# Batch 1 of a Fourier-mixing and ELU kernel in the quarter form, with another order of the first 17 steps

## The chip, the cores and the metric

The kernel runs on one core of one Trainium2 chip. The metric is the device time of one execution in microseconds. A profile of one execution on the chip, with a trace of every instruction, goes with it. In the text PE is TensorE (matmuls), DVE is VectorE, ACT is ScalarE, POOL is GpSimd, and SP is the engine that issues most transfers.

## The reference

```python
batch, seq, dim = (8, 3008, 256)
X = np.fft.fft(x, axis=1)
X = np.fft.fft(X, axis=2)
y = X.real.astype(np.float32).reshape(8 * 3008, 256)
h = y @ w_in                              # 256 x 2048
g = np.where(h > 0.0, h, np.exp(np.minimum(h, 0.0)) - 1.0)
out = (g @ w_out).astype(np.float32)      # 2048 x 256
```

The real part of a two-dimensional Fourier transform of every batch, and then a two-layer network with ELU between its layers. All of it is float32.

## The kernel before

**What is computed, and in what pieces.** The transform is symmetric, so only half of its rows (1504 in a batch) are made, as a real part (`Rr`, with one channel kept apart in `Rb`) and an imaginary part (`Ir`); each of them gives two tokens, h+ and h−. The channel part of the transform is folded into the first weight matrix: `fold_chunk` multiplies w_in by cosines and sines, chunk by chunk (eight chunks, 256 of the 2048 hidden columns each), into `Wc` and `Ws`. `Rr`, `Ir` and `Rb` are rings of columns in SBUF which the transform fills and the main loop reads. The middle channel's weights, one row of `Ws`, are needed as columns, `wex`: `spread_last_row` takes them there by two SP transfers through DRAM, `turn_last_row` and `put_last_row` by two one-column matmuls against the tile `pick` and an ACT copy.

**The main loop.** A tile is 256 ring columns, and has eight steps, one for each chunk. Step i is: P (`mm_P`, two matmul instructions of Wc by Rr into a PSUM bank of the tag H), E on DVE (`even_part`, L1352, `Rb * wex + H` into SBUF, in two halves), Q (`mm_Q`, Ws by Ir onto the same bank, so that H becomes h+), h− on DVE (L1366, `2E − H`), the ELU of both (b+ and b− and x+ and x− on ACT; g+ and g− on DVE, L1382), four sums on GpSimd (L603, G<-G), and the matmuls of the second layer into pA to pD. From the third tile on these are a Winograd form of seven products (X1, X2, X3); in the first 16 steps they are plain (Xa, Xb). Three banks have the tag H, and transforms and folds use them too.

**The transform of a batch.** It has four parts (real and imaginary, even and odd k), each in an even and an odd half. Batches 0 and 1 use the class `Dft`: rows of x in four tiles `xl0` to `xl3` (128 x 1536, `load_x`), folded on GpSimd by `mirror_folds` (30 operations for batch 1), then a matmul half of three instructions with 128 rows (`dft_mms`), of 189 columns for an even half and 377 for an odd one. Batches 2 to 7 use the class `Quarter`: the rows come in two sets, near and far, 96 and 94 rows of four (`load_quarter` with indirect transfers, `load_odd`), go through `mirror_sum`, `half_sum` (on DVE), `channel_fold`, `channel_edge`, and then `quarter_pairs`, `shift_pairs` and `turn_pairs` (on DVE, with the table `twist_tab`), and each half is four instructions with 94 or 95 rows and columns. `at_quarter` places a transform of that form: two halves, then the step at which its far part is finished and the step at which its even and odd half are joined.

**The extra channel.** One channel of all eight batches is transformed by itself: `load_ext` and `get_ext` bring it, `fold_ext` folds it, `dft_ext` (24 matmul records) transforms it, four ACT copies `ext_side` take it from PSUM, `ext_unfold`, `ext_rows`, `ext_up` and `ext_down` unfold it, and `spread_ext` puts it into the rings by SP transfers through DRAM.

**What sets the order.** `at(t, fn)` files an operation under a time t; all are sorted by t and issued in that order. A step is T = `PERIOD` = 4.8 long in these times. Operations on the compute engines are pinned to the order of the program; transfers on SP that are not pinned may be moved by the scheduler. The order until about step 7 is a list written out, `FRONT`, with short names: P4 is P of step 4, f3 the fold of chunk 3, Wc3 and Ws3 ACT's copies of that fold out of PSUM, J a part of batch 0's last transform, w3… and u3… the conversions of weight chunks. The words of a line are filed 0.001 apart.

Of the kernel before, what the change touches and what calls it, by code (L numbers as in the profile page):

```python
# [9 lines left out]
FP = mybir.dt.float32  # L10
# [167 lines left out]
def kernel(  # L178
# [381 lines left out]
    def load_quarter_mats(ri, kodd):  # L560
        t = cpool.tile([128, BW], FP, tag=f"MC{ri}{kodd}", name=f"QM{ri}{kodd}")
        QM[ri, kodd] = t
        n = sum(QW[i % 2] for i in range(2 * ri + kodd))
        nc.sync.dma_start(
            out=t[0:96, 0 : QW[kodd]], in_=QM_dr.ap()[:, n : n + QW[kodd]]
        )
# [166 lines left out]
    def mirror_folds(L):  # L733

        ops = []
        rows = [t.rearrange("p (m d) -> p m d", d=ND) for t in L]
        for j, k in ((3, 2), (0, 1)):
            own, other = rows[j], rows[k][:, ::-1]
            for m in range(6):
                ops.append(  # L740
                    lambda own=own, other=other, m=m: gtt(
                        own[:, m, 1:], own[:, m, 1:], other[:, m, :0:-1], ALU.add
                    )
                )
            ops.append(
                lambda own=own, other=other: gtt(
                    own[:, :, 0:1], own[:, :, 0:1], other[:, :, 0:1], ALU.add
                )
            )
        EO = [None] * 4  # L750
        for kodd in range(2):
            z = L[1 + kodd]
            for n in range(4):
                c = slice(384 * n, 384 * n + 384)
                ops.append(
                    lambda z=z, c=c, kodd=kodd: gtt(
                        z[:, c], L[0][:, c], L[3][:, c],
                        ALU.subtract if kodd else ALU.add,
                    )
                )  # L760
            for ri in range(2):
                t = EO[2 * ri + kodd] = spool.tile(
                    [128, 768], FP, tag=f"{'eo'[ri]}{1 + 2 * kodd}", bufs=1, name="eo"
                )
                for h in range(2):

                    def fold(z=rows[1 + kodd], t=t, ri=ri, h=h):
                        src = z[:, 3 * h : 3 * h + 3]
                        lo, hi = (
                            v.rearrange("p m (d o) -> p m o d", o=2)  # L770
                            for v in (src[:, :, 1:129], src[:, :, 255:127:-1])
                        )
                        o = t[:, 384 * h : 384 * h + 384]
                        o = o.rearrange("p (m o d) -> p m o d", o=2, d=64)
                        if ri:
                            gtt(o, lo, hi, ALU.subtract)
                        else:
                            gtt(o, lo[:, :, ::-1], hi[:, :, ::-1], ALU.add)

                    ops.append(fold)  # L780
                if not ri:
                    o = t.rearrange("p (m o d) -> p m o d", o=2, d=64)
                    state["edge", kodd] = lambda o=o, z=rows[1 + kodd]: act(
                        o[:, :, 0, 63:64], z[:, :, 0:1]
                    )
        return EO, ops

# [12 lines left out]
    def half_sum(kodd, far, h):  # L800

        n = 94 if far else 96
        a, b, o = (lines(j, far)[0:n] for j in (0, 3, 1 + kodd))
        for m in (2 * h, 2 * h + 1):
            vtt(o[:, 3 - m], a[:, m], b[:, m], ALU.subtract if kodd else ALU.add)
# [440 lines left out]
    def ext_side(g, rows=NB):  # L1246
        kodd, par = EXT[g]
        n = NO if kodd else NE if par else 2 * NH
        t = spool.tile([128, 384], FP, tag="side", bufs=2, name="side")
        act(t[0:rows, 0:n], state["ext"][32 * g : 32 * g + rows, 0:n])  # L1250
        state["side", par] = t

    def ext_unfold(kodd, tt, rows=NB):
        n = NO if kodd else NE
        h = (n + 1) // 2
        even = state["side", 0]
        a = spool.tile([128, NE], FP, tag="bs", bufs=BS, name="bs")
        unfold(a, even, even[:, h : 2 * h], rows, n, tt)
        state["es"] = a[0:rows]

    def ext_rows(kodd, tt, rows=NB):
        n = NO if kodd else NE
        if not kodd or rows < NB:
            rx = spool.tile([128, HALF + 1], FP, tag="rx", bufs=1, name="rx")
            state["rx"] = rx[0:rows]
        rx, a, b = state["rx"], state["es"], state["side", 1][0:rows]
        o, base = 1 - kodd, kodd * RUN
        m = n - 2 * o
        tt(rx[:, base : base + n], a[:, 0:n], b[:, 0:n], ALU.add)
        top = base + RUN - 1  # L1270
        tt(rx[:, top : top - m : -1], a[:, o : o + m], b[:, o : o + m], ALU.subtract)
        if not kodd:
            tt(rx[:, HALF:], a[:, 0:1], b[:, 0:1], ALU.subtract)
            nc.sync.dma_start(
                out=r4_dr.rearrange("o b -> b o"), in_=rx[:, HALF : HALF + 1]
            )
        nc.sync.dma_start(
            out=r128_dr[0:rows, base : base + RUN], in_=rx[:, base : base + RUN]
        )

    def ext_up():
        rx = state["rx"] = spool.tile(
            [128, HALF + 1], FP, tag="rx", bufs=1, name="rx"
        )[0:NB]
        a, b = state["es"], state["side", 1][0:NB]
        vtt(rx[:, 0:NE], a, b[:, 0:NE], ALU.add)
        vtt(rx[:, HALF:], a[:, 0:1], b[:, 0:1], ALU.subtract)

    def ext_down():
        rx, a, b = state["rx"], state["es"], state["side", 1][0:NB]  # L1290
        vtt(
            rx[:, RUN - 1 : RUN - 1 - (NE - 2) : -1],
            a[:, 1 : NE - 1], b[:, 1 : NE - 1], ALU.subtract,
        )
        nc.sync.dma_start(
            out=r4_dr.rearrange("o b -> b o"), in_=rx[:, HALF : HALF + 1]
        )
        nc.sync.dma_start(out=r128_dr[0:NB, 0:RUN], in_=rx[:, 0:RUN])
# [398 lines left out]
    def open_x(b):  # L1697
        state["L"], state["loads"] = load_x(b)

# [47 lines left out]
    names["L"] = lambda: [open_x(1)] + [state["loads"][n]() for n in (4, 5)]  # L1747
    for n in range(4):
        names[f"L{n}"] = lambda n=n: state["loads"][n]()
    for slot in range(8):  # L1750
# [10 lines left out]
        (-20.84, "e3 o3"),  # L1761
        (-19.11, "w0a w0b w0p w0R c3"),
        (-17.62, "w0s w0M"),
        (-16.21, "e0a e2b o2"),
        (-14.32, "e2a o0 c2"),
        (-12.89, "E2 f0 O2"),
        (-11.63, "xl1 xs e1 x-even"),
        (-9.8, "e0b c1 o1 c0 x-odd x-copy Wc0"),
        (-8.58, "E0 Ws0 EO0"),
        (-7.29, "wm0 wex0 O0 R-odd"),  # L1770
        (-5.76, "w1b EO2"),
        (-4.55, "w2b R-even u0b w2d u0a EO1 w1d"),
        (-3.25, "I-odd R-copy w1l w1a x-sum u0l"),
        (-1.92, "w1R R-sum w1p I-even x-down R-up"),
        (-0.64, "Irc2 w1s u0p P0 x-up I-copy w1M"),
        (0.82, "R-down O-even Irc I-sum u1l V0"),
        (2.21, "w1P w2l P1 I-up u0d"),
        (3.48, "I-down Q0 u0R R4 V1"),
        (4.76, "f1 h0 b+0 O-copy u0s Q1"),
        (5.99, "x+0 w2a b-0 u0M O-odd"),  # L1780
        (7.24, "Wc1 g+0 x-0 O-sum Ws1"),
        (8.46, "w2R w2p h1 wm1 g-0 b+1 P2"),
        (9.82, "wex1 O-down b-1 w2s Xa0 x-1 V2 w2M x+1"),
        (11.32, "O-up w3l Q2 g-1 w2P g+1 Xb0"),
        (12.61, "h2 u1a b-2 EO3 u1p f2"),
        (14.06, "u1b x-2 w3a P3 u1d w3b u1s b+2 Xa1 L"),
        (15.24, "L0 V3 x+2 Ws2 g-2 w3d u1R Q3 g+2"),
        (16.44, "w3p u3b Wc2 Xb1 b+3 w3R h3"),
        (17.88, "w4b b-3 J-even u1M w4l w3s x-3"),
        (19.2, "P4 x+3 u2l u2b w3M Xa2 u3d V4"),  # L1790
        (20.51, "w4d g-3 u2d w3P Q4 g+3 J-copy"),
        (21.72, "w4a Xb2 b+4 u2R J-sum w4p h4"),
        (23.12, "x+4 f3 u2a L1 P5 g+4 Ws3"),
        (24.53, "u2p w4R Xa3 V5 b-4 u3l"),
        (25.78, "u2s x-4 Q5 u2M g-4"),
        (27.2, "Xb3 h5 b+5 u3R Wc3 u3a x+5"),
        (28.7, "b-5 P6 w4s u3p L2 J-odd x-5"),
        (30.87, "V6 w4M Xa4 g+5"),
        (32.25, "u3s L3 Q6 w4P g-5 Xb4 b+6 h6 J-up J-down u3M"),
        (33.32, "b-6"),  # L1800
# [33 lines left out]
    for c, t in ((2, 15.2435), (3, 23.1265)) + tuple((c, (2 * c - 1) * T + 0.04) for c in range(4, 8)):  # L1834
        at(t, lambda c=c: spread_last_row(c))
# [291 lines left out]
```

## Time and profile before

| | |
|---|---|
| median of 4 runs | 1908.23 us (1907.2 to 1908.85) |
| profiled execution, its own time | 1907.66 us |
| its span in the profile | 1905.8 us |
| granted TensorE clock | 1.00 |
| PE busy | 1897.6 us (100% of the span) |
| weight loads (PEld) busy | 1647.1 us (86%) |
| DVE busy | 1488.1 us (78%) |
| POOL busy | 1352.9 us (71%) |
| ACT busy | 879.6 us (46%) |

A row of the table is one engine's busy time in one execution. The page also holds the chain of work that ended last, followed back from the last instruction; the list of waits says for which engine TensorE stood idle; the timeline lists instructions in order of time, with the idle time before each and what ended it; and the view of a tile lists all operations that read or write it. A float32 matmul instruction appears as two records in the trace.

### The profile page before, as it was taken

What the parts mean: (1) busy time and instruction counts of PE and PEld (TensorE: products, weight loads), DVE (VectorE), ACT (ScalarE), POOL (GpSimd) and SP (SyncE); (2) the same over time, 40 slices, a digit from 0 to 9 for tenths busy, and PEclk for the clock granted to TensorE, in tenths of its full rate; (3) what the DMA queues carried; (4) which work ended last, traced back from release to release, by engine and by line L of the source; (5) the groups of instructions that cost most, each with busy time, mean ns of one, the idle gap of its engine ahead of it and who ended that gap; (6) DMA issues with size and microseconds to landing.
All of it is one profiled execution on the core that took longest, in us unless ns stands there. A gap on an engine that the chain in (4) does not pass through costs nothing.

```text
span 1905.8 us, 27983 instructions
## 1 busy us (share of the span) xinstructions
PE 1897.6 (100%) x8972; PEld 1647.1 (86%) x8972; DVE 1488.1 (78%) x2836; ACT 879.6 (46%) x1723; POOL 1352.9 (71%) x1846
## 2 busy tenths in 40 slices
PE   9999999999999999999999999999999999999999
PEld 6888888888888888888888888888888888888887
DVE  8766667888878888778877788877888778777666
ACT  5754444444444444444444444444444444444443
POOL 4887668786677766777667777687766777556664
PEclk9999999999999999999999999999999999999999
DMA  8146211211011110111101111022110210100101
GB/s 340 45 33 37 60 24 46 52 24 36 12 44 41 32 34 12 45 41 30 31 20 49 35 27 30 13 55 44 24 24 16 55 20 15 17 12 15 20 12 23
DMA packets 278934, 73.66 MB, mean 39 GB/s; under 512 B 254402, under 2 KB 268998, under 8 KB 278788
## 3 DMA queue, kind: packets, MB, share of 16 engines
q1 hardware_dynamic: 270148, 61.44, 15.9%
q0 software_dynamic: 6464, 10.18, 1.7%
q8 instruction: 71, 1.16, 0.3%
q14 instruction: 75, 0.61, 0.1%
q10 hardware_dynamic: 2176, 0.26, 0.1%
HBM read 46.96 MB, written 24.80 MB: 38 GB/s over the span
## 4 chain that ended last, share of the span: by engine, by line
PE 96%; DVE 2%; DMA 1%; ACT 1%; issue 0%; POOL 0%; ACTq 0%; POOLq 0%; DVEq 0%
PE H L594 37%; PE pB L594 17%; PE pC L594 17%; PE pD L594 17%; PE pA L594 9%; DMA xl<-in_x_dram,ix 0%; DVE e L691 0%; DVE E L1352 0%; DVE o L691 0%; DVE pow L462 0%; POOL w L603 0%; ACT Wsc L606 0%; ACT G L606 0%; ACT M L606 0%; DMA wex<-wx 0%
## 5 line engine op out<-in xcount | busy, mean ns | idle before, releaser
L603 POOL TENSOR_TENSOR G<-G 128x256 f32<-128x256 f32 x1437 | 1047.6, 738 | 496.5 <-DVE G L1382 341.8
L606 ACT ACTIVATE G<-H 128x512 f32<-128x512 f32 x376 | 224.5, 597 | 917.5 <-DVE G L1366 913.9
L1352 DVE SCALAR_TENSOR_TENSOR E<-Rb,wex,H 128x256 f32<-128x256 f32 x752 | 327.6, 477 | 310.7 <-PE H L594 304.1
L594 PE MATMUL H<-Rr,Wsc 128*128 128x256 f32 x1504 | 388.0, 380 | 0.5 <-ACT Wsc L606 0.5
L594 PE MATMUL H<-Ir,Wsc 128*128 128x256 f32 x1504 | 386.8, 380 | 1.2 <-DVE E L1352 1.2
L594 PE MATMUL pC<-G,WT 128*128 128x256 f32 x1440 | 369.5, 379 | 0.0
L594 PEld LDWEIGHTS H<-Ir,Wsc 128*128 128x128 f32 x1504 | 278.5, 189 | 49.0 <-DVE E L1352 3.7
L594 PEld LDWEIGHTS H<-Rr,Wsc 128*128 128x128 f32 x1504 | 281.6, 190 | 41.6 <-issue 2.3
L594 PEld LDWEIGHTS pC<-G,WT 128*128 128x128 f32 x1440 | 273.6, 190 | 37.2
L1366 DVE SCALAR_TENSOR_TENSOR G<-E,H 128x512 f32<-128x512 f32 x376 | 257.0, 683 | 45.1 <-POOL G L603 11.9
L1382 DVE SCALAR_TENSOR_TENSOR G<-G,H 128x512 f32<-128x512 f32 x376 | 255.9, 680 | 39.8 <-ACT G L606 39.8
L1382 DVE SCALAR_TENSOR_TENSOR G<-M,G 128x512 f32<-128x512 f32 x376 | 256.8, 683 | 0.7 <-ACT M L606 0.7
L606 ACT ACTIVATE G<-G 128x512 f32<-128x512 f32 x376 | 233.4, 621 | 0.0
L594 PE MATMUL pA<-G,w 128*128 128x256 f32 x784 | 229.4, 379 | 0.0
L594 PE MATMUL pB<-G,w 128*128 128x256 f32 x784 | 229.3, 379 | 0.0
L594 PE MATMUL pD<-G,w 128*128 128x256 f32 x784 | 229.3, 379 | 0.0
L606 ACT ACTIVATE M<-G 128x512 f32<-128x512 f32 x376 | 223.9, 596 | 2.8 <-DVE G L1366 2.8
L606 ACT ACTIVATE M<-M 128x512 f32<-128x512 f32 x376 | 221.1, 588 | 0.1
L594 PE MATMUL pB<-G,WT 128*128 128x256 f32 x720 | 214.6, 380 | 0.0
L594 PE MATMUL pD<-G,WT 128*128 128x256 f32 x720 | 214.1, 379 | 0.0
L594 PEld LDWEIGHTS pA<-G,w 128*128 128x128 f32 x784 | 148.9, 190 | 20.8 <-DVE G L1382 0.3
L594 PEld LDWEIGHTS pB<-G,w 128*128 128x128 f32 x784 | 148.9, 190 | 20.4 <-PE H L594 0.2
(171 smaller groups left out, 1583.6 us busy)
## 6 DMA issues: line engine op xcount, KB each, us to landing
out_dram<-ot SPq DMA_DIRECT2D x496, 32.0 KB
xq<-in_x_dram SPq DMA_DIRECT2D x48, 94.0 KB
out_dram<-ot SPq DMA_DIRECT2D x256, 2.0 KB
Rb<-r SPq DMA_DIRECT2D x10, 376.0 KB
raw<-in_moe_w_in_dram SPq DMA_DIRECT2D x7, 512.0 KB
MC<-dft_mats SPq DMA_DIRECT2D x3, 943.5 KB
xq<-in_x_dram SPq DMA_DIRECT2D x12, 192.0 KB
xq<-in_x_dram SPq DMA_DIRECT2D x36, 64.0 KB
```

The source lines that it names most:

```text
L594: nc.tensor.matmul(out_, lhsT=lhsT, rhs=rhs, start=start, stop=stop, skip_group_check=True)
L603: pin(nc.gpsimd.tensor_tensor(out=o, in0=a, in1=b, op=op))
L606: pin(nc.scalar.activation(out=o, in_=i, func=func, **kw))
L1352: nc.vector.scalar_tensor_tensor(out=S.E[:, c], in0=Rb[:, cols(i)], scalar=wex[:, f : f + 1], in1=S.H[:, c], op0=ALU.mult, op1=ALU.add,)
L1366: nc.vector.scalar_tensor_tensor(out=two(S.G[:, 0:512])[:, :, ::-1], in0=two(S.E), scalar=2.0, in1=two(S.H), op0=ALU.mult, op1=ALU.subtract,)
L1382: nc.vector.scalar_tensor_tensor(out=o, in0=e, scalar=-1.0, in1=h, op0=ALU.add, op1=ALU.max)
```

## The change

Batch 1 leaves the class `Dft` for the class `Quarter`. `mirror_folds`, `open_x`, `at_half`, `at_dft` and `begin_folds` go. `load_quarter` and `load_odd` of batch 1's near rows are filed at 3.078 and behind it (the loads before stood at 14.06 and behind it), and a list of some 80 operations with a time for each takes the place of the loops. Batch 1's half sums run on DVE, as those of the later batches do.

The four matrices of the quarter form go together into the tiles of the old matrices MC10 and MC11, at 7.2 T (before: one by one at 51 to 60 T).

The extra channel is transformed two steps later; its four ACT copies stand together in step 32 (before: two in step 30 and two in step 33).

The last row of the chunks 6 and 7 is turned by two one-column matmuls and an ACT copy each, as that of chunk 1 is, in place of two transfers.

`FRONT` is a new list. On TensorE the order differs in three places: Q1 stands before the fold f1, P3 before f2, and J-odd (the odd half of batch 0's last transform) before P6. On DVE, ACT, GpSimd and SP many operations of the first steps change places.

Instructions of the two programs: PE 4557 and 4569, DVE 2838 and 2912, ACT 1733 and 1741, POOL 1851 and 1863, SP 1581 and 1605.

```diff
-    def load_quarter_mats(ri, kodd):
-        t = cpool.tile([128, BW], FP, tag=f"MC{ri}{kodd}", name=f"QM{ri}{kodd}")
...
+    def load_quarter_mats():
+        n = 0
+        home = [
+            cpool.tile([128, BW], FP, tag=f"MC1{i}", name=f"QM{i}") for i in range(2)
+        ]
...
-    def half_sum(kodd, far, h):
+    def half_sum(kodd, far, h, tt):
...
-            vtt(o[:, 3 - m], a[:, m], b[:, m], ALU.subtract if kodd else ALU.add)
+            tt(o[:, 3 - m], a[:, m], b[:, m], ALU.subtract if kodd else ALU.add)
...
-    names["L"] = lambda: [open_x(1)] + [state["loads"][n]() for n in (4, 5)]
+    names["L"] = lambda: [
+        fn(1, j, 0) for j in (3, 0) for fn in (load_quarter, load_odd)
+    ]
...
-        (3.48, "I-down Q0 u0R R4 V1"),
-        (4.76, "f1 h0 b+0 O-copy u0s Q1"),
-        (5.99, "x+0 w2a b-0 u0M O-odd"),
...
-        (12.61, "h2 u1a b-2 EO3 u1p f2"),
-        (14.06, "u1b x-2 w3a P3 u1d w3b u1s b+2 Xa1 L"),
...
-        (27.2, "Xb3 h5 b+5 u3R Wc3 u3a x+5"),
-        (28.7, "b-5 P6 w4s u3p L2 J-odd x-5"),
...
+        (3.078, "I-down L V1 Q0 h0 u0s w2a"),
+        (4.940, "Q1 R4 O-copy b+0 b-0 u0R f1 x+0"),
...
+        (12.168, "Xb0 h2 u1a b-2 u1p P3 w2P w3b"),
+        (13.774, "f2 u1b x-2 u1d b+2 w3a Ws2 Xa1 EO3 x+2 u1s w3d"),
...
+        (26.276, "u2M Q5 Xb3 h5 b+5 Wc3 u3a J-odd"),
+        (27.968, "w4s"),
+        (28.624, "b-5 x-5 P6"),
...
-    for c, t in ((2, 15.2435), (3, 23.1265)) + tuple((c, (2 * c - 1) * T + 0.04) for c in range(4, 8)):
+    for c, t in ((2, 15.2435), (3, 23.1265)) + tuple((c, (2 * c - 1) * T + 0.04) for c in (4, 5)):
         at(t, lambda c=c: spread_last_row(c))
+    for c in (6, 7):
+        at((2 * c - 1) * T + 3.02, lambda c=c: turn_last_row(c))
+        at((2 * c - 1) * T + 3.03, lambda c=c: put_last_row(c))
...
-    at(29 * T + 4.75, dft_ext)
-    at(30 * T + 1.46, lambda: ext_side(0))
-    at(30 * T + 1.47, lambda: ext_side(1))
...
-    at(33 * T + 1.46, lambda: ext_side(2))
-    at(33 * T + 1.47, lambda: ext_side(3))
...
+    at(31 * T + 4.75, dft_ext)
+    at(32 * T + 1.46, lambda: ext_side(0))
+    at(32 * T + 1.47, lambda: ext_side(1))
+    at(32 * T + 1.48, ext_open)
+    for g in (2, 3):
+        at(32 * T + 1.49, lambda g=g: ext_side(g))
+    at(10.0, quarter_table)
+    at(7.2 * T, load_quarter_mats)
...
-    for step, ri, kodd in ((26, 0, 0), (34, 1, 0), (37, 0, 1), (42, 1, 1)):
-        at_dft(step, 2, 1, ri, kodd, lambda k=2 * ri + kodd: state["EO"][k])
...
+    for t, fn, *key in (
+        (23.22, mirror_sum, 3, 0, 1),
+        (26.00, quarter_row, 1),
...
+        (39.33, half_sum, 1, 0, 0, vtt),
+        (44.10, half_sum, 0, 0, 0, vtt),
+        (44.12, half_sum, 0, 0, 1, vtt),
+        (44.52, channel_fold, 0, 0, 0, 0),
+        (44.52, half_sum, 1, 0, 1, vtt),
...
+        (131.63, quarter_pairs, 1, 0, 0, 1),
...
+        (139.46, turn_pairs, 1, 0, 'y'),
...
+        (155.20, ext_unfold, 0, vtt),
+        (156.21, ext_up, 0, vtt),
+        (157.11, ext_down, 0, vtt),
...
+        (292.04, spread_ext, 1, 1),
+    ):
+        at(t, lambda fn=fn, key=key: fn(*key))
+
+    for step, ri, kodd, finish, join in ((28, 0, 0, 0, 31), (34, 1, 0, 0, 37), (38, 0, 1, 42, 53), (44, 1, 1, 50, 54)):
+        at_quarter(step, 1, ri, kodd, finish, join)
```

## The prediction

> **What bounds the kernel now.** I read the chain that ended last first, then what TensorE waits for. From the page, shares of the span on the chain:
>
> ```profile
> PE 96%; DVE 2%; DMA 1%; ACT 1%; issue 0%; POOL 0%; ACTq 0%; POOLq 0%; DVEq 0%
> ```
>
> TensorE's waits, all in this list (engine, line, who is waited for, us, times, longest):
>
> ```profile
> PE H L594 <- DVE E L1352: 1.2, 3, 0.7
> PE H L594 <- ACT Wsc L606: 1.2, 2, 0.6
> PE M L594 <- DVE zero L581: 1.1, 1, 1.1
> PE H L594 <- ACT mid L606: 0.7, 1, 0.7
> PE pC L594 <- DVE xe L600: 0.7, 1, 0.7
> PE pB L594 <- DVE e L691: 0.2, 1, 0.2
> ```
>
> They come to 5.1 us of 1905.8 (PE is busy 1897.6). A microsecond of TensorE work taken out is a microsecond of time, unless another engine becomes late at that place; work on DVE, ACT, GpSimd or a queue counts only where it makes TensorE wait. So the sum goes: TensorE work out, TensorE work in, stalls that go, stalls that come. Prices come from the timeline (start us, us busy, engine, line, instructions; in brackets idle before and releaser). I take gaps from start to start: the first matmul behind a stall shows 0.11 us more than its neighbours, which the idle time leaves out.
>
> **1. Batch 1's transform (gain).** Old form, then the form that batch 2 has already:
>
> ```profile
> 173.13 1.44 PE L594 MATMUL H<-MC,eo 128*128 128x189 f32 x6
> 174.41 0.81 PE L594 MATMUL H<-Rr,Wsc 128*128 128x256 f32 x3
> ...
> 184.77 2.07 PE L594 MATMUL H<-MC,eo 128*128 128x377 f32 x6
> 186.68 0.59 PE L594 MATMUL H<-Rr,Wsc 128*128 128x256 f32 x2
> ```
>
> ```profile
> 431.82 0.36 PE L594 MATMUL H<-QM,e 95*128 95x95 f32 x2
> 432.01 0.39 PE L594 MATMUL H<-QM,o 94*128 94x95 f32 x2
> 432.24 0.39 PE L594 MATMUL H<-QM,e 94*128 94x95 f32 x2
> 432.46 0.39 PE L594 MATMUL H<-QM,o 94*128 94x94 f32 x2
> 432.68 1.06 PE L594 MATMUL H<-Rr,Wsc 128*128 128x256 f32 x4
> ```
>
> An old even half holds TensorE for 174.41 − 173.13 = 1.28, an old odd half for 186.68 − 184.77 = 1.91. The other three of each kind are 1.27 to 1.28 and 1.90, so four transforms cost 12.7. A quarter half costs 432.68 − 431.82 = 0.86, and the slot's first matmuls behind it .04 more (0.90 for 0.86): 0.90. Eight of them: 7.2. **−5.5.** The saving does not follow the columns: 189 columns take 0.213 per record (1.28 / 6), 377 take 0.318, 95 take 0.108. [...]
>
> **2. Last rows of chunks 6 and 7 by TensorE (cost).** Chunk 1 does it this way now: its four one-column records run 34.97 to 35.44, 0.47, and the next matmul is .09 late: 0.55. Twice: 1.1. They also wait for ACT's put of the folded chunk. Chunk 7's put ends at 108.57 where TensorE is through with its Q at 108.34, so +0.35; chunk 6's ends at 94.60, Q at 96.15, no wait. Bounds 0.9 to 1.9, taken **+1.4**. The two SP transfers that go were off the path, except at one place (3c).
>
> **3. Stalls that go.** (a) P6 at 59.95 waited for ACT's chunk of Wc (0.55 idle; .82 start to start). In the new order J-odd's 1.9 us stand ahead of P6, which covers it: −0.8. (b) The one-column matmuls of chunk 1 waited 0.61 for ACT; O-copy goes earlier into idle ACT time: −0.2 (0 to −0.8). (c) Q12's E at 112.10 waited for wex by DMA, which chunk 7 no longer uses: −0.48. (d) At 215.43 (0.31 idle, .74 start to start with refill) E had been held through exp+ by two ACT copies of 0.98 at 209.78; these leave the step: −0.7. The one at 101.33 (0.71, GpSimd's weights, .98 start to start) I leave standing; GpSimd's work between the weight products of these steps falls from 27.0 to 23.0 us, summed from its rows, so it may go too. Together **−2.2** (−1.3 without b and d, −3.2 with 101.33).
>
> **4. Stalls that come.** TensorE tolerates a late E by about 0.65 us in the first 16 slots and about 0.2 later (Q starts 2.6 and 2.16 after P, E could start at 1.07 and takes 0.87). What is new on DVE:
>
> ```profile
> L600 DVE TENSOR_TENSOR xq<-xq,xq x96: 484/746/951, 245.4 to 1545.9; 96x256 f32<-96x256 f32 x48, 94x256 f32<-94x256 f32 x48
> ...
> DMA to landing us min/median/max: 3.2/6.2/10.0
> ```
>
> ```profile
> 87.72 0.87 DVE L1352 SCALAR_TENSOR_TENSOR E<-Rb,wex,H 128x256 f32<-128x256 f32 x2 [2.89 <-PE H L594]
> ```
>
> - Slot 9/10: six half sums stand between E9 and g+9, so ahead of E10. At 0.40 to 0.87 (the row less .08 overlap) that is 2.4 to 5.2; the idle 2.89 that DVE had there covers most, and P10 waits for an H bank that g+8 frees, behind them. 0 to 1.5, taken 0.3.
> - Slot 32: four ext copies on ACT together (4 × .49 = 1.96, where two and two stood) and the unfold and sums of the extra channel on DVE (.6 to .9 each): slot sum 5.7 on DVE for 4.75 on TensorE. 0 to 1.1, taken 0.6.
> - Slot 37: two turns (0.35 / 0.71 / 0.88) before g+36, so sum_2 on GpSimd and X1 are late. DVE 5.5 for 4.75. 0 to 1.5, taken 0.4.
> - Slots 42 and 50: DVE 5.1 for 3.9 with X3 deferred; slack 1.1. 0 to 0.8, taken 0.3.
>
> **+1.6** (0 to 4.9). The half sums read two SBUF tiles while GpSimd runs, and the row's spread from 484 to 951 ns is that encounter; DVE operations with a PSUM source (xq<-H,near, 243 to 250) have none. [...]
>
> **At nothing.** The extra channel's TensorE part (24 records, 191.52 to 193.54) only moves two slots. The new mirror sums and channel folds on GpSimd (0.72 to 0.84 each) replace 30 old ones (mean 0.94); by rows its total stays, 1333.9 to 1333.3 us, and its 29% idle hides it; without that cover each would be late for a G sum of 0.73. DVE gets 36 us more, hidden by its 418 us of idle outside the slots above. The x loads of batch 1 now issue from 3.078 on, in the first 50 us, where the DMA share is 0.94 (0 to 20) and 0.81 (20 to 50); the four QM matrices follow at 7.2 steps and are first used at step 28. What these loads pass on SP is the second rival.
>
> **Sum.** −5.5 + 1.4 − 2.2 + 1.6 = −4.7 from the profiled execution's 1907.66: 1902.96. That execution stands 0.57 under the median 1908.23, so I forecast **1903.5**. The terms' own bounds: with every old stall gone and no new one −8.2, with the new ones at their ends −1.4 (worked below).
>
> **Rivals.**
> *DVE turns late at the five slots* (chance 0.20). If the half sums, turns and ext sums run at their upper prices, term 4 is 4.9: −5.5 + 1.4 − 2.2 + 4.9 = −1.4, 1906.8. For: DVE's sums exceed TensorE's in these slots. Against: batches 2 to 7 carry the same operations, and none of the listed waits lies between 216 us and the tail.
> *The SP queue* (chance 0.12, the slower one). SP issues in order, and the program lets a transfer wait for the one eight places ahead of it. In the new order wex of chunk 2 stands behind x loads that wait for an indirect load's landing, wex of chunk 3 behind the QM loads, wex of chunk 5 behind two far loads that only the last half sum releases. E4, E6 and E10 need them. If landings take the row's 10.0 instead of 6.2, each is 3.8 late, less 0.65 of tolerance: 3 × 3.15 = 9.5, so −4.7 + 9.5 = +4.8, 1913.0. For: the DMA share of 0.81 to 0.94 until 50 us. Against: only one E that held TensorE waited for wex now, and TensorE lost 0.2 there. It decides from about 7 us of landing in the first 60 us.
> *No new stalls, and 101.33 goes too* (chance 0.13): −5.5 + 1.1 − 3.2 and all of (b), 0.6 more: −8.2, 1900.0. For: GpSimd has 4 us less to do there. Against: slot sums of term 4.
>
> **Numbers.** Forecast case 0.55, with its own range 1901.5 to 1905.5. The whole range takes in the third rival with 0.8 below it (0.9 for 1.1 in term 2, and the small unlisted gaps), the first with 1.5 above it (the bounds of terms 2 and 3), and leaves the second out: 1899.2 to 1908.3. What a measurement of this kernel can tell from no change is about 0.2%, 3.8 us: faster means under 1904.4. Of the forecast case five parts in six lie there, and the third rival: 0.46 + 0.13 = 0.59. Slower over 1912.0 is two thirds of the second rival: 0.08. The rest 0.33.
>
> **What would show it.** TensorE busy down from 1897.6 by about 4 (−5.5 and +1.1); eight halves of 0.86 at slots 28 to 45; no wait at P6, none of wex at chunk 7; two more pairs of one-column matmuls near 95 and 109 us. Wrong if waits for E with releaser DMA wex appear before 60 us, or waits for DVE or GpSimd of over 1 us in slots 9, 10, 32, 37, 42 or 50, or if a quarter half costs over 1.0.

## The result, and the profile after

The kernel after takes 1909.49 us in the median of 40 runs (1907.77 to 1916.65). The kernel before, in 60 runs beside it, takes 1907.67. The ratio of the means is 1.0013, 95% interval 1.0009 to 1.0018 (here and below a ratio is one of means, which long runs pull up more than the median). So it is slower by 0.13%, which is less than the 0.2% that I had set as the least that counts, but it stands 6.0 above the forecast of 1903.5 and outside the range. The profiled execution took 1907.92, span 1906.0, granted clock 1.00.

The chain that ended last, shares by engine:

```profile
PE 91%; DMA 3%; DVE 2%; SPq 1%; issue 1%; POOL 1%; ACT 0%; ACTq 0%; DVEq 0%; POOLq 0%
```

TensorE's share fell from 96% to 91%, and DMA and SP's queue stand in the chain, where the queue had nothing before. Busy PE fell from 1897.6 to 1894.8, yet the span did not follow. TensorE's waits (engine, line, who is waited for, us, times, longest), the two rows that grew:

```profile
PE H L600 <- DVE E L1292: 4.5, 5, 2.3
...
PE pB L600 <- POOL G L609: 0.8, 1, 0.8
```

Waits for E rose from 1.2 to 4.5, a wait of X1 for GpSimd's sums is new, and the two waits for ACT's `Wsc` (1.2) are gone. A quarter half of batch 1 in the timeline (start us, us busy, engine, line, instructions):

```profile
188.12 0.36 PE L600 MATMUL H<-QM,e 95*128 95x95 f32 x2
...
188.99 1.06 PE L600 MATMUL H<-Rr,Wsc 128*128 128x256 f32 x4
```

It holds TensorE for 0.87 and its neighbour for .04, 0.9 as priced. Where the gain went is seen from the start of each step's E, after minus before, in us:

| step | 3 | 5 | 6 | 7 | 8 | 9 | 10 | 12 | 15 to 26 | 30 | 37 | 38 | 45 | 50 |
|---|---|---|---|---|---|---|---|---|---|---|---|---|---|---|
| later by | −.40 | .67 | 2.82 | .36 | 1.14 | 2.20 | 4.73 | 4.60 | 4.58 | .12 | 1.57 | 1.40 | −.68 | .21 |

From step 3 to step 15 the kernel lost 4.98. From step 26 to the end it won back 4.37. (At step 30 the extra channel's 2.2 are missing, since they stand two steps later.) The loss is made by VectorE in steps 7 to 10:

```profile
72.88 1.51 DVE L408 TENSOR_SCALAR pow<-raw 128x512 int32<-128x512 int32 x1
...
76.50 2.29 DVE L606 TENSOR_TENSOR xq<-xq,xq 96x256 f32<-96x256 f32 x2
...
83.33 2.09 DVE L606 TENSOR_TENSOR xq<-xq,xq 96x256 f32<-96x256 f32 x6
...
86.54 1.66 DVE L462 SCALAR_TENSOR_TENSOR pow<-raw,pow 128x512 int32<-128x512 int32 x1
...
88.73 1.34 DVE L408 TENSOR_SCALAR pow<-raw 128x512 int32<-128x512 int32 x1
89.99 1.49 DVE L420 TENSOR_SCALAR w<-raw 128x512 int32<-128x512 int32 x1
92.44 0.87 DVE L1292 SCALAR_TENSOR_TENSOR E<-Rb,wex,H 128x256 f32<-128x256 f32 x2 [0.96 <-DMA wex<-wx]
```

Two half sums in step 8 took 2.29 and six in step 9 took 2.09. The three weight operations of step 9 took 1.66 + 1.34 + 1.49 = 4.49, where they had taken 0.68 + 0.42 + 0.95 = 2.05. Those in the kernel before, and the three folds of batch 1 that GpSimd ran beside them:

```profile
82.33 0.68 DVE L462 SCALAR_TENSOR_TENSOR pow<-raw,pow 128x512 int32<-128x512 int32 x1
...
83.54 0.42 DVE L408 TENSOR_SCALAR pow<-raw 128x512 int32<-128x512 int32 x1
83.87 0.95 DVE L420 TENSOR_SCALAR w<-raw 128x512 int32<-128x512 int32 x1
```

```profile
82.36 3.04 POOL L603 TENSOR_TENSOR xl<-xl,xl 128x255 f32<-128x255 f32 x3
```

From E9 to E10: 2.09 of sums and 2.44 of longer weight operations, less the 2.89 of idle time that was there, plus 0.96 of waiting for `wex`, is 2.6; measured is 2.53. From E8 to E9: 2.29 of sums and 0.2 net of weight operations less 1.30 of idle time, 1.2; measured 1.06. What GpSimd did goes with both lengths of the sums. It ran beside the two, and it stood still beside the six:

```profile
77.03 1.48 POOL L609 TENSOR_TENSOR w<-raw,w 128x512 f32<-128x512 f32 x1
...
86.36 1.30 POOL L609 TENSOR_TENSOR w<-raw,w 128x512 f32<-128x512 f32 x1 [4.36 <-ACT w L612]
```

VectorE in the same 28 us, before and then after (the window in us, its length, busy time with instructions of each engine, clock, DMA share, GB/s):

```profile
68.00:96.00 28.00, 28.00 (x133) 23.25 (x133) 21.97 (x39) 22.09 (x42) 23.12 (x24) 1.00 0.01 1
```

```profile
68.00:96.00 28.00, 24.93 (x115) 19.60 (x114) 26.87 (x42) 18.25 (x34) 17.96 (x18) 1.00 0.03 8
```

VectorE (third of the engines) went from 21.97 to 26.87 of 28 and sets the time there. TensorE, full before, is busy 24.93.

The 0.96 for `wex` is the order on SP: the two far loads stand between the two transfers of chunk 5.

```profile
84.47 0.22 SPq L649 DMA_DIRECT2D wx<-Wsc  x1
85.90 1.32 SPq L336 DMA_DIRECT2D xq<-in_x_dram  x2
87.31 0.40 SPq L652 DMA_DIRECT2D wex<-wx  x1
```

### The profile page after: what moved, and what is told of

Same layout as the page of the kernel before. It is cut to its first block, busy times and chain, and to the rows that moved or that the text cites. A ratio compares the mean times of both kernels' runs of the same rounds, so it can differ in the third digit from the quotient of the medians.

```text
span 1906.0 us, 28161 instructions
## 1 busy us (share of the span) xinstructions
PE 1894.8 (99%) x8996; PEld 1645.6 (86%) x8996; DVE 1519.5 (80%) x2910; ACT 880.5 (46%) x1731; POOL 1355.3 (71%) x1858
## 4 chain that ended last, share of the span: by engine, by line
PE 91%; DMA 3%; DVE 2%; SPq 1%; issue 1%; POOL 1%; ACT 0%; ACTq 0%; DVEq 0%; POOLq 0%
PE H L600 35%; PE pB L600 16%; PE pC L600 16%; PE pD L600 16%; PE pA L600 8%; DMA x<-in_x_dram 1%; DMA xq<-in_x_dram 1%; SPq L1527 1%; DMA wx<-Wsc 0%; DMA xl<-in_x_dram,ix 0%; DMA wex<-wx 0%; DVE E L1292 0%; SPq L1133 0%; DVE G L1322 0%; DVE e L697 0%
```

## The experiments

Beside each group of runs the kernel before had a median of 1906.97 to 1907.53. The "loss" is E15 less E3 against before, 4.98 in the kernel after. Stalls of 2.25 us and more are in many of these runs followed by a stretch in which TensorE's clock is halved (0.50 in windows of e1, e2, e4 and e6; see the last section), so some runs stand further off than their stalls add up to. Waits of TensorE are idle times in the profiled execution.

My theories were that the half sums make VectorE late in steps 8 to 10, that SP's order makes `wex` late at E6 and E10, and that the moved extra channel delays batch 2's loads and so X1 at step 36.

**e5: the new FRONT alone, in the kernel before.**

```diff
-        (4.76, "f1 h0 b+0 O-copy u0s Q1"),
+        (4.940, "Q1 R4 O-copy b+0 b-0 u0R f1 x+0"),
...
-        (28.7, "b-5 P6 w4s u3p L2 J-odd x-5"),
+        (28.624, "b-5 x-5 P6"),
```

> The kernel before with the new FRONT and nothing else of the change (batch 1 in the old form, its loads at the new places, all last rows but chunk 1's by SP). Theory B+A (batch 1's new work on DVE, GpSimd and SP in steps 6 to 12 makes the loss): the step that feeds E15 starts at or before the 116.79 us of the kernel before, since the wait of P6 (0.55) goes, and the whole is 0 to 1.2 us faster than before. Rival F (the new order of FRONT itself makes the loss): E15 is 2 us or more late here too.

1908.05, ratio 1.0003 (0.9994 to 1.0012). The wait at P6 is gone and E15 stands 0.25 earlier, though 0.47 is lost between steps 3 and 15 (TensorE waits 0.34 at E4). The new list by itself gives nothing and costs nothing.

**e6: the old FRONT in the kernel after,** with batch 1's loads at their new times.

```diff
-        (4.940, "Q1 R4 O-copy b+0 b-0 u0R f1 x+0"),
+        (4.76, "f1 h0 b+0 O-copy u0s Q1"),
...
+        (3.079, "L"),
```

> The changed kernel with the FRONT of before (batch 1's loads stay at their new times). Theory B+A: E15 is still 3 to 5 us later than before's 116.79 and the whole within 1.5 us of the changed kernel. Rival F: E15 is within 1 us of before, and the whole is about 4 us faster than the changed kernel.

1916.62, ratio 1.0044 (1.0031 to 1.0058); the loss is 10.0, some 2.2 of it from half a clock between 54.8 and 59.2. On SP the x loads stand between `wx` (43.30) and `wex` (49.96) of chunk 2, and E4 waits 4.7. So the early loads of the quarter form are dear beside the old list, and the two parts belong together.

**e1: the QM loads behind `wex` of chunk 5.**

```diff
-    at(7.2 * T, load_quarter_mats)
+    at(10.5 * T, load_quarter_mats)
```

(with each of the four loads pinned there)

> The changed kernel with the four QM loads issued on SP behind the wex transfers of chunk 5 instead of in front of and behind chunk 3's. Theory A (SP queue and its transfers): wx of chunk 3, 6.44 us to land at 55.26 in the changed kernel, lands in under 3.5; the wait of E6 for wex (2.54 on DVE, 1.19 from start to start on TensorE instead of 0.21) goes; about 1.0 us less than the changed kernel if nothing else becomes late. Theory B (DVE itself is late in steps 8 to 10 through half sums and slowed weight operations): E6 comes early but the time to E10 stays, under 0.4 us less.

1911.92, ratio 1.0026 (1.0017 to 1.0036). `wx` of chunk 3 lands 3.0 after its issue in the place of 6.4, the 2.54 that VectorE waited before E6 is gone, and E9 stands where it stood against E3 (2.65 for 2.60). So the wait at E6, the most visible one on VectorE, cost nothing net: it was made up before E8. At E10 the QM loads now follow `wex` of chunk 5, TensorE waits 3.05, and half a clock follows (0.50 from 96 to 99 us).

**e2: the far loads behind `wex` of chunk 5.**

```diff
-                nc.sync.dma_start(
+                load = nc.sync.dma_start(
...
+                if far and b == 1:
+                    pin(load)
```

> The changed kernel with the far loads that stand between wx and wex of chunk 5 held back behind wex. Theory A: wex of chunk 5 is issued before 87 and lands in 2.3 instead of 5.0; E10, which waited 0.96 on DVE for it, starts about 1.0 us earlier, and the kernel is 1.0 us faster. The rest of E10's 2.55 us on TensorE is not wex and stays at about 1.5 us: theory B, DVE busy without a gap from E8 to 91.5. If A alone is the cause of E10's lateness, the whole 2.4 goes.

1909.59, ratio 1.002 (1.0009 to 1.0031). The wait of E10 falls from 2.27 to 1.22, and E11 and E12 wait 0.72 and 1.18: loss 5.5. SP's order added to the wait at E10 but was not the whole of its cause. This profiled execution (1919.38) also shows what a long run is made of, on ACT:

```profile
205.35 0.41 ACT L614 ACTIVATE xq<-xq 1x256 f32<-1x256 f32 x1 [8.89 <-DMA xq<-in_x_dram]
```

`quarter_row` of batch 2 waits 8.89 for its row, the ELU of the step stands behind it on ACT, and TensorE stands for 5.3 us at 202.1.

**e3: the half sums on GpSimd.**

```diff
-        (44.10, half_sum, 0, 0, 0, vtt),
+        (44.10, half_sum, 0, 0, 0, gtt),
```

(all four near ones)

> The changed kernel with the eight operations of batch 1's four near half sums on GpSimd instead of DVE. Theory B: E9 (0.68 over) and E10 (2.44 over) come on time except for wex, 1.5 to 2 us less by step 10; GpSimd's weight products get up to 8 x 0.73 = 5.8 us later and may give some of it back at E12. Theory A: E10 still waits for wex until 92.4, so less than 1 us changes.

1911.08, ratio 1.0023 (1.0009 to 1.0037). E10 comes in time, and GpSimd is late instead: the half sums stand ahead of its weight product `raw`, and TensorE waits 2.4 for that at the fold of a chunk.

```profile
96.86 1.13 PE L600 MATMUL H<-raw,CC 128*128 128x256 f32 x4 [2.41 <-POOL raw L609]
```

Loss 5.4: the work moved, and the wait moved with it.

**e10: eight folds and one mirror sum of batch 1 later,** with far loads that wait for them.

```diff
-        (44.52, channel_fold, 0, 0, 0, 0),
+        (60.0, channel_fold, 0, 0, 0, 0),
...
-        (76.02, mirror_sum, 0, 1, 0),
+        (90.00, mirror_sum, 0, 1, 0),
```

> The changed kernel with eight channel folds of batch 1 on GpSimd moved out of steps 9 to 14 to steps 12.5 to 13.6 of the order, the far loads that wait for them and the first far mirror sum with them; the half sums stay. Theory B (DVE operations with two SBUF sources wait whole GpSimd operations out): the two stretched weight operations behind E9 and E10 (1.66 and 0.93 to 2.4 instead of 0.68) shrink, E10 loses 1 us of its 2.44, E12 its wait for GpSimd (0.79); E15 1 to 2 us earlier. If only wex holds E10, nothing moves.

1916.38, ratio 1.0045 (1.0031 to 1.0058). TensorE waits 0.39 at E12 in the place of 0.63, but GpSimd is busy for 46.9 of the 50 us from 100 on, and TensorE waits 0.75 (for E), 0.43 (for a weight) and 1.36 (for sums) between 118 and 142 us. E10 still waits 2.4.

**e7: batch 1 as a whole later.**

```diff
+        t += 12.0 if 39 < t < 77 else 8.0 if 77 < t < 105 else 4.0 if 105 < t < 130 else 0.0
         at(t, lambda fn=fn, key=key: fn(*key))
```

> The changed kernel with batch 1's half sums, channel folds and far loads and sums filed later: 12 units of the order's time for those filed at 39 to 77, 8 for 77 to 105, 4 for 105 to 130. That takes them out of steps 8 to 10, where DVE and GpSimd also turn weights. Theory B: the waits of E8, E9 and E10 (0.45, 0.68 and 2.44 us over on TensorE) shrink to under 1.5 together, E15 is 2 to 3.5 us earlier than the changed kernel's 121.36. Theory A alone: only wex's share of E10 goes, 1.0. Risk: the far loads reach SP later and push the extra channel and batch 2 still further back, so that the wait at X1 of step 36 grows.

1927.43, ratio 1.011 (1.0095 to 1.0126). This order does not compute the reference's result, so only its waits are read. Steps 8 to 10 are as before the change, and the half sums stop TensorE in step 12 instead (3.6). Later X1 waits up to 7.7 for mirror sums that wait for far loads. So the half sums can't simply go later: the far loads that wait for them go later too.

**e8: batch 2 three steps later.**

```diff
-            at((r0 + step) * T + dt, lambda: fn(*key))
+            d = 3 if b == 2 and (step > 6 or fn is mirror_sum) else 0
+            at((r0 + d + step) * T + dt, lambda: fn(*key))
```

> The changed kernel with batch 2's mirror sums, and all that follows in batch 2, three steps later (its near loads where they are). Theory C (GpSimd's G sums of step 36 stand behind a mirror sum of batch 2 that waits for a load queued on SP behind 48 stores): the wait of X1 at 235 (0.8 us in the changed kernel's profile, 2.5 to 3.4 in the four runs since) goes, no clock drop follows it, and the median falls by 1 to 3 us. If the sums are late for another reason (turns on DVE before g+), the wait stays.

1923.17, ratio 1.0079 (1.0065 to 1.0093). The wait of X1 at step 36 falls to 0.46, and eight new waits for E of 0.5 to 1.7 stand between 270 and 590 us, where batch 2's work meets batch 3's.

**e4: the extra channel's loads earlier.**

```diff
-            (15.2 + 0.5 * n) * T,
+            (14.4 + 0.5 * n) * T,
...
-    at(29.0 * T, get_ext)
+    at(27.0 * T, get_ext)
```

> The changed kernel with the loads of the extra channel where they stood before (load_ext from 14.4 steps, get_ext at 27); its transform stays two steps later. Theory A: the channel's loads no longer hold SP until 196 and the x loads of batch 2 come earlier, so GpSimd's mirror sum at 232 no longer waits 3.8 us, and the 0.83 us that TensorE waits for GpSimd's sums at 235.09 goes: about 1.0 us less. Rival C: batch 2's loads wait for batch 1's tiles, which the quarter form of batch 1 holds longer, and the stores that stand in front of them; then the wait at 235 stays and so does the time.

1912.86, ratio 1.0029 (1.0017 to 1.004). X1 still waits 2.6, and `dft_ext` waits 1.1 for GpSimd. But the loads did not come forward: filed earlier, they were issued from 127.77 on, and the last four from 185.31 to 193.84, for 181.92 to 187.98 in the kernel after. So this run does not test whether earlier loads would help.

**e9: the consumers of batch 2's rows two steps later, and the extra transform one step later.**

```diff
-    at(31 * T + 4.75, dft_ext)
+    at(32 * T + 4.75, dft_ext)
...
-        rel(4, 3.0, quarter_row, b)
+        rel(*((6, 1.2) if b == 2 else (4, 3.0)), quarter_row, b)
```

(and four mirror sums of batch 2 two steps later)

> The changed kernel with three consumers of late SP transfers moved behind the landings, and no transfer moved: ACT's copy of batch 2's first row (quarter_row) two steps later, the last four of batch 2's near mirror sums two steps later, the extra channel's fold and transform one step later. Theory C (in steps 28 to 38 engines that issue in order, ACT and GpSimd, stand at the head of their queues for loads that SP issues late, behind the extra channel's slow loads): the waits of TensorE at X1 of step 36 and at the extra channel's transform go, nothing stays between 200 and 245 us but the 0.3 of step 32; per batch-1 and extra-channel part of the trace, E49 stands at most +0 against the E15 of the same run less 4.4; median 1.5 to 3 us below the changed kernel's, fewer runs with a clock below 1.000. Rival: the waits come from DVE being late (turns) and stay.

1911.89, ratio 1.0026 (1.0016 to 1.0036). The wait for `xe` is gone and that of X1 falls to 0.46. The extra transform one step later brings four others between 207 and 224 us (0.72, 0.88, 1.04, 0.38).

**e13: the consumers alone.**

```diff
-        rel(4, 3.0, quarter_row, b)
+        rel(*((6, 1.2) if b == 2 else (4, 3.0)), quarter_row, b)
...
-                rel(start + n, 1.3, mirror_sum, (0, 3)[n % 2], far, (0, 2, 1, 3)[n // 2])
+                rel(start + n + (2 if b == 2 and not far and n > 3 else 0), 1.3, mirror_sum, (0, 3)[n % 2], far, (0, 2, 1, 3)[n // 2])
```

> As e9 without the step for the extra channel: only ACT's copy of batch 2's first row and four of its near mirror sums two steps later. Theory C: no wait of TensorE for GpSimd's sums at step 36 (0.8 to 3.4 us so far), E49 at E15 less 5.4 (against less 4.4 in the changed kernel), the waits of e9 at 207 to 223 us (0.9, 1.0, 1.2, 0.5) absent but for 0.4 at step 32; the extra channel's transform can still wait 1 to 2 us. Median 1 to 2 us below the changed kernel's.

1910.3, ratio 1.0014 (1.0005 to 1.0023). The long wait at step 36 falls to 0.47. From step 15 to step 49 this run wins 3.56, with 0.98 lost at `dft_ext` for GpSimd's `xe`; its loss to step 15 is 6.15, with half a clock behind the stall at E10 (0.999 in the mean of the execution).

**e11: e9 with the far loads pinned and chunk 6's last row by SP again; e12: the same with e10's folds.**

```diff
-    for c in (6, 7):
+    for c in (7,):
...
+                if far and b == 1:
+                    pin(load)
```

> As e9, and also the far loads behind wex of chunk 5 (as in e2) and the last row of chunk 6 by SP again instead of TensorE. By the sum: 1.0 less at E10 of which the DVE/GpSimd pair gives some back by E12, and 0.55 less for the one-column matmuls of chunk 6: 0.5 to 1.5 us below e9. Rival A: wex of chunk 6 by SP is late and E12 waits more than now.

1911.57, ratio 1.0026 (1.0017 to 1.0035), loss 5.46. Without chunk 6's pair of one-column matmuls TensorE waits 1.61 at E12 for 1.18 in e2 (loss 5.49): with VectorE as late as it is, that pair costs nothing to be seen.

> e11 and e10 together. If the parts add up: E15 2 us and the rest 1.5 to 3 us better than the changed kernel, a median of about 1905, below the kernel before. If the pair's work only moves, E13 to E16 take back what E10 gains, about 1907.

1912.28, ratio 1.0029 (1.0018 to 1.0041). E13 is only 2.8 late, but E19 is 6.1 late: what step 12 gained is given back between 115 and 139 us.

**e14: e13 and e2 together.**

```diff
+                if far and b == 1:
+                    pin(load)
...
+        rel(*((6, 1.2) if b == 2 else (4, 3.0)), quarter_row, b)
```

> e13 with the far loads behind wex of chunk 5 as in e2. Theory B (the DVE/GpSimd pair sets the time of E13): as e13 within 0.5 us, but without the long wait at E10 (2.4 to 3.2 us) and so without the clock drop that followed it in some runs: fewer slow runs. Theory A: 1 us better than e13. Either way about 1907, level with the kernel before or up to 1 us below it.

1908.37, ratio 1.0013 (1.0003 to 1.0022); profiled 1907.29 with no wait over 1.4 us after the first 20. The loss is still 5.5.

**e15: without the near half sums of batch 1,** and **e16: without its near mirror sums too.** Both leave these operations out.

```diff
+        if fn is half_sum and not key[1]:
+            continue
```

```diff
+        if fn in (half_sum, mirror_sum) and not key[1]:
+            continue
```

> The changed kernel without the four near half sums of batch 1 (eight operations on DVE, so batch 1's transform is not the reference's). Counted from E3, E15 loses 5.0 us to the kernel before in the changed kernel and 0.5 with FRONT alone. Theory B: without them the loss to E15 falls by 1.5 to 2.5 us (E9 on time, E10's wait only wex). Theory A: it falls by under 0.7, wex at E6 and E10 being the cause.

1905.06, ratio 0.9995 (0.9985 to 1.0005), with six of ten runs at 1903.8 to 1905.2. The loss falls from 4.98 to 1.37, so the half sums cost 3.6. This holds what they do to SP's order as well, since the far loads now go out at 69.12 and 79.43, ahead of chunk 5's `wx`; e2 mended that order alone, and its loss stayed at 5.5. E9 and E10 are then as far apart as before, 7.37, although the weight operations are still long (0.69, 1.50 and 1.87 in step 9):

```profile
84.67 1.50 DVE L408 TENSOR_SCALAR pow<-raw 128x512 int32<-128x512 int32 x1
86.09 1.87 DVE L420 TENSOR_SCALAR w<-raw 128x512 int32<-128x512 int32 x1
88.57 0.87 DVE L1292 SCALAR_TENSOR_TENSOR E<-Rb,wex,H 128x256 f32<-128x256 f32 x2 [0.61 <-PE H L600]
```

They take 4.06 together without the sums, 4.49 with them, and 2.05 in the kernel before. So of the 2.44 by which they grew 2.0 is not the sums' doing, and of the 2.89 of idle time that VectorE had in this slot only 0.61 is left for them.

> e15 also without batch 1's eight near mirror sums (ten operations of GpSimd, 6 to 7 us, in steps 4 to 8 and one later). Theory B: a further 1 to 1.5 us by E15, since the weight operations at E7 and E8 (1.5 us instead of 0.43 to 0.95) are no longer stretched; what is left of the 5.0 is then the one-column matmuls (1.1 to 1.5) and wex at E10. Theory A: E15 as in e15.

1910.78, ratio 1.0015 (1.0003 to 1.0028). Without anything that held them back, the far loads went to SP in front of `wex` of chunk 3, and E6 waited 3.7. From step 7 to step 13 little more was lost (6.06 to 6.2 late), but with E6 so late this does not price the mirror sums: what they add in the kernel after stays open.

**e17: the half sums spread** over steps 8 to 11, in e14, one pair to a step.

```diff
-        (39.33, half_sum, 1, 0, 0, vtt),
-        (44.10, half_sum, 0, 0, 0, vtt),
-        (44.12, half_sum, 0, 0, 1, vtt),
+        (39.33, half_sum, 0, 0, 0, vtt),
+        (47.10, half_sum, 0, 0, 1, vtt),
...
+        (51.90, half_sum, 1, 0, 0, vtt),
...
+        (56.32, half_sum, 1, 0, 1, vtt),
```

> The computation is whole. As the run with the mirror-row consumers two steps later and the far loads behind the extra rows, with the near half sums of batch 1 (3.6 us at steps 8 to 10 by the run that left them out) in four places of one pair each, from step 7 to step 11, and one fold behind them. Theory A (the half sums cost what they cost because they stand together): the stretch between step 3 and step 15 loses about 3 us in the place of 5 and the median is about 1.5 us under that of the run without the spread, near 1906.5, below the kernel before. Theory B (VectorE and GpSimd together are full from step 8 to step 13, wherever the sums stand): the wait is met at steps 11 to 13 by folds and sums that come late, the loss stays 4.5 to 5.5, and the median is 1908 to 1910.

1909.13, ratio 1.0008 (0.9999 to 1.0017), loss 6.5. Spreading made it worse, since every pair now ran, wholly or in part, beside GpSimd (VectorE's timeline):

```profile
88.09 3.29 DVE L608 TENSOR_TENSOR xq<-xq,xq 96x256 f32<-96x256 f32 x2
```

The longest is shown; the four pairs take 2.29, 3.29, 2.23 and 1.82. The same eight sums take 9.63 where they had taken 2.29 + 2.09 = 4.38. That gave the next theory: their price is set by GpSimd, not by their number.

**e18: e14 with the first pair in GpSimd's pause,** behind E7.

```diff
+        (34.53, half_sum, 1, 0, 0, vtt),
         (39.32, mirror_sum, 3, 0, 2),
-        (39.33, half_sum, 1, 0, 0, vtt),
```

> The computation is whole. As the run with the mirror-row consumers two steps later and the far loads behind the extra rows (e14), with only the first pair of near half sums moved, from behind E8 to behind E7, where GpSimd stands idle for 3.7 us. Theory A (a half sum costs what it costs by whether GpSimd runs beside it: the six in GpSimd's pause of step 9 took 2.09 together, .35 each, the pairs beside GpSimd 2.2 to 3.3): the pair takes 0.7 to 0.9 in the place of 2.29, E9 waits no more (1.06 between E8 and E9 goes, E8 is .3 to .7 later), the loss between step 3 and step 15 is 4.5 to 5.1 in the place of 5.5, and the median about 1907.7, level with the kernel before. Theory B (a half sum is dear wherever it stands, or the weight operations behind it stretch by as much as it saves): the pair takes 1.5 or more or E8 comes over 1 us later, the loss stays at 5.3 or above, and the median at 1908.4.

```profile
69.94 0.75 DVE L608 TENSOR_TENSOR xq<-xq,xq 96x256 f32<-96x256 f32 x2
...
82.02 2.09 DVE L608 TENSOR_TENSOR xq<-xq,xq 96x256 f32<-96x256 f32 x6
```

The same pair takes 0.75 in the place of 2.29. E9 starts 5.70 behind E8 (5.76 before the change), and the loss is 4.05 for e14's 5.5. The profiled execution took 1906.21, and five of twelve runs 1905.97 to 1906.30, below the lowest run of the kernel before beside them (1906.69). But four lie at 1913.8 to 1915.2, and the median is 1907.66 against 1907.22, ratio 1.0013 (1.0001 to 1.0024): the best of the versions that compute the whole, and no faster than before. What the four long runs wait for was not traced.

## Why the prediction was wrong, by its steps

**Term 1, right in the number, wrong in the reason.** Eight halves of 0.9 for 12.7: −5.5 on record. The slots where old halves leave and new ones come, added up in the table's full form, give −5.55. But the sentence that the saving does not follow the columns misread the line. The timeline's line gives the form of its first record only. By form, the two even halves that begin with 189 columns are

```profile
L594 PE MATMUL H<-MC,eo 128*128 128x189 f32 x8 | 1.6, 323 | 0.0
...
L594 PE MATMUL H<-MC,eo 128*128 128x378 f32 x4 | 1.6, 480 | 0.0
```

So each half has four records of 189 columns and two of 378. At the rate of the 377-column ones (0.318) that is 4 × 0.159 + 2 × 0.319 = 1.27, so the old halves do go by their columns, and only the 95-column records (0.108) stand above their column time (0.080). What holds those at 0.108 no run shows. With the right column counts the columns give 1.27 a half and the same −5.5; the term took the measured gap, so its number stands.

**Term 2, a little high.** The slots of steps 11 and 14 are 0.37 and 0.41 longer, 0.8 together for 1.4, below the lower bound of 0.9, and of chunk 6's share nothing can be seen in the loss (e11).

**Term 3, right as far as it went.** No wait at P6 (e5 shows that the list alone removes it), chunk 1's pick waits 0.19 in the place of 0.77 (start to start), step 13 wins back 0.44 of the 0.48 for `wex`, and the stall at 215 is gone. The one at 101.33 stands (0.63 idle for 0.71), as taken.

**Term 4 failed, at "Slot 9/10: six half sums".** I gave it 0.3 with a bound of 1.5; it is 3.6 (e15). Three things in that sentence were wrong. It did not count the two sums of step 8, which alone made E9 1.06 later. It priced a sum at 0.40 to 0.87 wherever it stood, by the row's spread over a whole run; what counts is what GpSimd does beside it: 0.35 to 0.38 in a pause (e18), 0.9 to 1.65 beside it (e17), as means over a group. And it took the 2.89 us that VectorE stood idle in the old trace as cover. The six ran in a pause and took only 2.09, less than the lower end I gave, but without them only 0.61 of that cover was left (e15), because the three weight operations of the slot take 4.06 in the place of 2.05. In the kernel before GpSimd ran folds beside those, three in 3.04; in the kernel after it runs weight products of 1.30 and 1.46 and folds of 2.17 for two. That GpSimd's other work is what lengthens them is read from these timelines; no run changed it alone. For the sums the traces show more: in the kernel before each of the row's 96 sums begins beside a GpSimd operation and ends 0.28 behind the end of that operation, and in the kernel after the pair of step 8 ends at 78.79, 0.28 behind the GpSimd product that ends at 78.51. My upper price came from the row's maximum of 0.951. But that row starts at 245.4, and GpSimd's last operation of 128x512 elements starts at 116.65 in the kernel before, so it held no sum beside one of them. The pairs of e17, which met GpSimd operations of 0.8 to 1.5, average 1.2 a sum.

**The SP rival** was seen at two of its three places. At E6 its price was nothing net (e1). At E10 it was one part of a wait that VectorE made: 1.05 less at E10 without it (e2), all of it met again by step 12. The half sums and the queue are one chain there, as I had written: the last half sum releases the far loads, and it does so just when `wex` needs the queue.

**"At nothing" failed in one sentence, that the extra channel's TensorE part "only moves two slots".** That part does; its loads move too, which I did not cost. They start on SP at 128.87, where they had started at 110.14, and the last four are issued from 181.92 to 187.98, where it had been 170.42 to 177.35. They are made of tiny packets, 5507 for 0.05 MB, as the queue's line for 180 to 190 us shows (packets, MB, share of the 16 engines' time):

```profile
q1 hardware_dynamic: 5507, 0.05, 69.6%
```

The time of these packets is 70% of what the 16 engines have there. Batch 2's loads stand behind them, and a last one behind 48 stores:

```profile
181.92 6.06 SPq L1133 DMA_DIRECT2D x<-in_x_dram  x4
...
203.70 23.68 SPq L1527 DMA_DIRECT2D out_dram<-ot  x48
227.48 0.65 SPq L336 DMA_DIRECT2D xq<-in_x_dram  x1
```

Before, that last load was issued at 215.10. On GpSimd the G sums of X1 stand behind a mirror sum, which waits 3.79 for rows, and start when it is through, at 232.81:

```profile
231.97 0.89 POOL L609 TENSOR_TENSOR xq<-xq,xq 96x255 f32<-96x255 f32 x2 [3.79 <-DMA r<-rx]
232.81 3.03 POOL L609 TENSOR_TENSOR G<-G 128x256 f32<-128x256 f32 x4
```

(The releaser named is the transfer that landed last by the records; with this sum and its like two steps later the wait falls to 0.47, e13.) TensorE waits 0.83 there in this execution, 2.5 and 2.6 in those of e2 and e4. That the extra channel's loads are what makes that last load late is read from this order on SP alone; no run moved them (e4). Slot 37 was priced at 0.4 for VectorE's turns; of the 1.4 that it cost 1.0 has this other cause, and the rest is near the price. Slot 32 was 0.3 for 0.6, and slots 42 and 50 nothing.

**The sum.** Against the forecast for this execution, 1902.96, 4.96 are missing: from step 3 to 15 I had −0.8 + 1.4 − 0.48 + 0.3 = 0.4 and the trace has 4.98, which leaves 4.6; X1 brings 1.0 more; the smaller terms that came out below their price take 0.6 off. **The step from this execution to the median failed too.** I took 0.57, the trace's distance before; it was 1.57. Of 40 runs 15 are above 1910, of 60 before one. In the traced executions of that kind (e2, and e15's at 1911.88) ACT waits 8.89 and 8.28 us for batch 2's row.

**What stays open.** 1.37 of the loss remains without the half sums. At E9 it is 1.44 already, where the FRONT alone has 0.56; from E9 to E15, with both one-column pairs in it, nothing more is lost. The other 0.9 ahead of E9 has no run of its own. That a wait for batch 2's rows makes the long runs of the kernel after is an inference from two other kernels.

## What to carry to other kernels

Price a VectorE operation like the half sum by what GpSimd does in that very moment (here 0.35 to 0.38 in a pause, 0.9 to 1.65 beside it), not by its mean over the run. Before idle time of the old trace is taken as cover, ask what else in that slot will grow: here other operations took 2.0 of the 2.9. Before a price is worked out from a grouped line, see its records by form. When a part "only moves", cost its loads on every queue that it moves past, and look at the engines that wait for what then stands behind, as GpSimd did for 3.79. After filing a load earlier, see in the trace whether it was issued earlier. When each repair moves a wait without shortening it, as in e1 to e12, leave the suspect out once: that one run sized the cause.

## What the runs showed of the hardware

**Half a clock after a stall.** Windows of e4 (window, length, busy time with instructions of PE, PEld, DVE, ACT and POOL, granted clock, DMA share, GB/s):

```profile
95.00:96.00 1.00, 1.00 (x5) 0.80 (x4) 1.00 (x3) 0.00 (x0) 0.18 (x1) 0.61 0.03 8
96.00:97.00 1.00, 1.00 (x4) 0.82 (x3) 1.00 (x2) 0.69 (x2) 1.00 (x1) 0.50 0.00 0
```

The windows of 94 to 95 and of 96 to 97 us stand at 1.00 and 0.50, so a mean of 0.61 between them is 0.22 us at the first and the rest at the second. So in e4, after a stall of 2.76 that ended at 93.94, the clock was halved from 95.22 to 98.62 (0.69 over 98 to 99), 3.4 us, which costs 1.7 by an estimate from these two levels. In e6 (0.58 over 52 to 54, 0.50 until 59, 0.92 in the next) it was halved from 52.3, within a stall of 4.71, to 59.2, 6.8 us. The length of the stall alone does not decide: 2.27 at E10 brought such a stretch in e9 and none in the kernel after, 2.25 brought one in e10, and 2.41 (e3) and 2.64 (e4) none. What goes with it shows in the clock of all twenty traces. Within their spans it falls sixteen times, and within a trace the falls and rises are whole multiples of 3.41 us apart: e6 falls at 52.32 and again at 243.48 (0.74 over 243 to 244), 56 of them later. In the 3.41 us just ahead of each fall TensorE stood idle for 2.14 us (e4) to 3.41 (e15); it was 2.2 in e6, 2.3 in e1 and 3.3 in e2. Of the other stretches of that grid at full clock none holds more than 1.93 (e10, until 95.43); the kernel after has 1.89 (91.48 to 94.89), since its stall lies across two. So in these traces 2.14 us of idle time in one stretch went with a fall and 1.93 did not. What makes the grid no run shows.

**Integer operations stretch as well.** The weight operation with one source (`pow<-raw`, int32) takes 0.42 in a pause of GpSimd (67.75 in the kernel before). The one at 72.88 in the kernel after takes 1.51, as much as the half sums: it starts 0.07 behind a GpSimd product (72.81, 1.29 long) and ends 0.29 behind that product's end. Beside GpSimd it need not be slow: at 83.54 in the kernel before it takes 0.42, and there GpSimd's three folds take 3.04, where two take 1.41 at 66.13.
